# FFT mixing and squared-ReLU FFN on one core: a doubled filter block, swapped weights from DRAM, a longer lag of the inverse units and later loads

## The chip, the cores and the metric

The kernel runs on one core of one Trainium2 chip. The metric is the device time of one execution in microseconds (us). Shown in tables are the median of several runs and, apart from it, one profiled execution with its trace.

## The reference

The input x holds 8 batches of 3008 tokens with 256 channels. Each batch goes through a global filter: a real FFT along the tokens, a product with a complex filter of 1505 frequencies, and the inverse FFT. Its result is the input of an FFN with a hidden width of 2048:

```python
X = np.fft.rfft(x, axis=1)
Y = X * (filt_r + 1j * filt_i)[None, :, :]
y = np.fft.irfft(Y, n=x.shape[1], axis=1)
h = np.maximum(y.reshape(B * S, D) @ w_in, 0.0)
out = (h * h) @ w_out
```

## The kernel before

**The FFT as matrix products.** 3008 is 64 x 47. The forward transform takes two stages: `unit_a` (over 47, line 297) and `unit_b` (over 64, line 359). `unit_b` also multiplies by the filter on VectorE (line 378): the products of one psum tile with the real and the imaginary filter go side by side into `prod`. Real and imaginary parts stand in the two halves of the partitions. The inverse takes two stages more: `unit_p` (weights sSP, lines 411 and following) and `unit_y` (line 439). Between the stages of a batch the data are turned through DRAM: u is written to dU and read back as ut, ze is written to dZ and read back as zt (`write_u`, `read_u`, `read_z`).

**The FFN.** Tokens go in 47 groups of 512. A group has 8 steps. In step s, `ffn_g1` computes two of 16 hidden tiles, ScalarE takes the ReLU out of PSUM, and VectorE squares. The second product of a group runs in the 8 steps after, for the first and last group by `ffn_g2`, for all others by a seven-product scheme (`sums` on VectorE, `products` on TensorE).

**Order.** The order of the program is written by hand, and each engine works its queue in this order. TensorE, VectorE and ScalarE have one queue each. SP (SyncE) issues writes and reads of dU and dZ and the stores; POOL (GpSimd) issues the loads of x, filter and weights, and in later batches the additions prod<-prod (line 385).

**Batch 0, the prologue.** It is not interleaved with the FFN. Its first stage is done straight from wide tiles of x (`chunk_a0`), and the turn of u is done on TensorE (`turn_u`) with half of the evictions on VectorE. Twelve `unit_b` give twelve products. Every third of them (p % 3 == 0) reads the psum tile directly; the others read `ub`, a copy in f16 made by ScalarE (line 376). The products of batch 0 aren't added by POOL. Instead `unit_p0` (line 389) multiplies both halves of a product, with sSP and with `sSPx`, which is sSP with its two partition halves swapped; `sSPx` is made by four copies on VectorE (lines 699 and 700). There are six `unit_p0`, of two products each; number k-1 stands behind the `unit_b` of step k.

**The filter tile sF.** It is loaded in three blocks of columns: (0,6), (6,12) and (12,24). Partitions 0 to 63 come from DRAM, 64 to 127 hold a second copy: the real part as it is, the imaginary part with its sign turned (`turn_f`, line 241). The copy of the real part is made by VectorE for the first block (line 240) and by a transfer from SBUF to SBUF on SP for the other two (line 235).

**Later loads.** After w_in's first half, POOL issues three of the eight x loads of batch 1. `load_rest` (line 274) then makes POOL wait by copying one element of the first zt tile into `tiny`; behind this gate stand w_in's second half, five x loads and both halves of w_out. `fill` issues matmuls on zeros ahead of the first `unit_y`.

**The plan.** `fft_plan` (line 622) gives each unit of batches 1 to 7 a place in the FFN steps, in half steps. For batch 1 the numbers are steps counted from 0: `unit_a` from 1, `read_u` at 11, `unit_b` from 15 to 29, `unit_p` 4.5 later, `read_z` at 34, and `unit_y` 0 to 3 fixed at 38 to 39.5. Group 5, which begins at step 40, is the first that needs a token of batch 1. Units of batch 2 begin with `unit_b` at 47.5.

Of the kernel before, what the change touches and what calls it, by code (L numbers as in the profile page):

```python
# [102 lines left out]
def kernel(  # L103
# [73 lines left out]
    def load_x(b, k):  # L177

        c, i = divmod(k, 2)
        if i == 0:  # L180
            x16s[(b, c)] = p_x16.tile([96, 8, D], F16, tag="x16", name=f"x16_{b}_{c}")
        t = x16s[(b, c)][:, 4 * i:4 * i + 4, :]
        m = slice(8 * c + 4 * i, 8 * c + 4 * i + 4)
        if b + 1 < B:
            v = xrows[b * S:b * S + 96 * NM, :].rearrange("(p m) d -> p m d", m=NM)
            nc.gpsimd.dma_start(out=t, in_=v[:, m, :])
        else:
            v = xrows[b * S:b * S + S, :].rearrange("(p m) d -> p m d", m=NM)
            nc.gpsimd.dma_start(out=t[0:80], in_=v[0:80, m, :])
            nc.gpsimd.dma_start(out=t[80:94], in_=v[80:94, m, :])  # L190
# [34 lines left out]
    def load_f(c0, c1):  # L225

        for im, filt in enumerate((filt_r, filt_i)):
            v = filt[0:1504, :].rearrange("(j c) d -> j c d", c=47)
            a = max(c0, 1)
            nc.gpsimd.dma_start(out=sF[0:32, im, c0:c1, :], in_=v[:, c0:c1, :])  # L230
            nc.gpsimd.dma_start(out=sF[32:64, im, a:c1, :], in_=v[:, 47 - a:47 - c1:-1, :])
            if c0 == 0:
                nc.gpsimd.dma_start(out=sF[32:33, im, 0, :], in_=filt[1504:1505, :])
        if c0:
            nc.sync.dma_start(out=sF[64:128, 0, c0:c1, :], in_=sF[0:64, 0, c0:c1, :])

    def turn_f(c0, c1):

        if c0 == 0:
            nc.vector.tensor_copy(out=sF[64:128, 0, c0:c1, :], in_=sF[0:64, 0, c0:c1, :])  # L240
        nc.vector.tensor_scalar_mul(out=sF[64:128, 1, c0:c1, :], in0=sF[0:64, 1, c0:c1, :],
                                    scalar1=-1.0)

    def load_const(t, d, k):
        c = slice(12 * k, 12 * k + 12)
        nc.gpsimd.dma_start(out=t[:, c, :], in_=d.ap().rearrange("p (a b) -> p a b", b=128)[:, c, :])

    def load_win(i):
        c = slice(1024 * i, 1024 * i + 1024)
        for k in range(2):  # L250
            nc.gpsimd.dma_start(out=sWin[:, k, c], in_=moe_w_in[128 * k:128 * k + 128, c])
# [4 lines left out]
                            in_=moe_w_out.rearrange("(jt r) c -> r jt c", r=128)[:, c, :])  # L256

    FC = ((0, 6), (6, 12), (12, 24))
    for k, i in ((0, 0), (1, 0), (0, 1), (1, 1), (2, 0), (2, 1)):
        load_wide(k, i)  # L260
    nc.sync.dma_start(out=sC1, in_=dC0.ap()[:, 704:896])
    load_const(sSB, dSB, 0)
    load_f(*FC[0])
    load_const(sSP, dSP, 0)
    load_f(*FC[1])
    load_const(sSB, dSB, 1)
    load_f(*FC[2])
    load_const(sSP, dSP, 1)
    load_win(0)
    for k in range(3):  # L270
        load_x(1, k)
    sSPx = [p_u.tile([128, 12, 128], F16, tag="u", name=f"sSPx_{k}") for k in range(2)]

    def load_rest():

        tiny = const.tile([1, 1], F16, name="tiny")
        nc.gpsimd.tensor_copy(out=tiny, in_=ztiles[0][0:1, 0, 0:1])
        load_win(1)
        for k in range(3, 8):
            load_x(1, k)  # L280
        for k in range(2):
            load_wout(k)

    def fill(n):

# [73 lines left out]
    def unit_b(b, p):  # L359
        if b == 0 and p % 4 > 1:  # L360
            ps = psO(f"psB_{b}_{p}").rearrange("p a d -> p (a d)")
        else:
            ps = psF(f"psB_{b}_{p}")
        for i in range(2):
            nc.tensor.matmul(ps[:, i * D:(i + 1) * D], sSB[:, 2 * p + i, :],  # L365
                             uts[b][:, 2 * p + i, :], start=True, stop=True)
        if b == 0:
            if p == 0:
                prods["ring"] = p_y.tile([128, 5, 2, 2, D], F16, tag="yt", name="prods_0")
            prod = prods["ring"][:, p % 5]  # L370
        else:
            prod = p_prod.tile([128, 2, 2, D], F16, tag="prod", name=f"prod_{b}_{p}")
        pv = ps.rearrange("p (a d) -> p a d", d=D)
        if b == 0 and p % 3:
            ub = p_prod.tile([128, 2, D], F16, tag="prod", name=f"ub_{p}")
            nc.scalar.copy(out=ub, in_=pv)
            pv = ub
        nc.vector.tensor_mul(  # L378
            out=prod,
            in0=pv.unsqueeze(1).to_broadcast([128, 2, 2, D]),  # L380
            in1=sF[:, :, 2 * p:2 * p + 2, :])
        prods[(b, p)] = prod
        if b > 0:
            for i in range(2):
                nc.gpsimd.dma_start(out=prod[64 * i:64 * i + 64, 0],  # L385
                                    in_=prod[64 - 64 * i:128 - 64 * i, 1],
                                    accum_op=mybir.AluOpType.add)
# [234 lines left out]
    def fft_plan():  # L622

        fixed, units, moves = [], [], []
        for b in range(1, B):
            f = (b * S // TG) * SLOTS - (48 if b > 1 else 40)
            d = 0
            if b == 1:
                for n in range(4, 16):
                    fixed.append(((n if n < 8 else n + 2 if n < 12 else 2 * n - 7) + n % 2 / 2,  # L630
                                  unit_y, 0, n))
                moves.append((7.5, read_z, 0, 3))
                for a in range(16):
                    fixed.append(((1 if a < 6 else 2) + a / 2, unit_a, b, a))
                moves.append((11, read_u, b))
                d = 7
            else:
                for a in range(16):
                    if a % 2 == 0 and b > 2:
                        moves.append((f + ((-57 + 2.3 * a) if b == 3 else (-66 + 2.75 * a)),  # L640
                                      load_x, b, a // 2))
                    units.append((f + (-16 + a, -46 + 2.1 * a, -56 + 2.75 * a)[min(b, 4) - 2],
                                  unit_a, b, a))
                moves.append((f + (4 if b == 2 else -6.5), read_u, b))
            for p in range(12):
                r = 15 + 14 * p / 11 if b == 1 else 7.5 + 26.5 * p / 11 if b == 2 else -2 + 36 * p / 11
                units.append((f + r, unit_b, b, p))
                if b == 1 and 2 <= p < 10:
                    moves.append((f + r, load_x, 2, p - 2))
                units.append((f + r + (4.5 if b == 1 else 7 - 2.5 * p / 11), unit_p, b, p))  # L650
            for c in range(4):
                moves.append((f + (40 + d / 7, 43, 48, 54)[c] - d, read_z, b, c))
            for n in range(16):
                (fixed if n < 4 else units).append((f + YN[n] - d, unit_y, b, n))
        work, used, done = {}, set(), {}
        for r, *u in fixed:
            h = int(2 * r)
            used.add(h)
            work.setdefault(h, []).append(u)
        rank = (unit_b, unit_p, unit_y, unit_a)  # L660
        for r, *u in sorted(units, key=lambda u: (rank.index(u[1]), u[0])):
            after = done.get((u[0], u[1]), -1)
            h = min((h for h in range(max(int(2 * r) - 3, after + 1), int(2 * r) + 12)
                     if h not in used),
                    key=lambda h: (sum(h + i in used for i in (-2, -1, 1, 2)) > 2) * 2
                    + abs(h - int(2 * r)))
            used.add(h)
            done[(u[0], u[1])] = h
            work.setdefault(h, []).append(u)
        for r, *u in moves:  # L670
            work.setdefault(int(2 * r), []).append(u)
        return work
# [12 lines left out]
    turn_u(0, nc.scalar, nc.vector)  # L685
    turn_u(1, nc.scalar, nc.scalar)
    turn_u(2, nc.scalar, nc.vector)
    for k in range(7):
        if k < 6:
            for p in (2 * k, 2 * k + 1):  # L690
                for c in FC:
                    if c[0] == 2 * p:
                        turn_f(*c)
                unit_b(0, p)
        if 0 < k < 4:
            turn_u(k + 2, nc.scalar, nc.vector)
        if k in (0, 3):
            c = slice(4 * k, 4 * k + 12)
            nc.vector.tensor_copy(out=sSPx[k // 3][0:64], in_=sSP[64:128, c, :])
            nc.vector.tensor_copy(out=sSPx[k // 3][64:128], in_=sSP[0:64, c, :])  # L700
        if k > 0:
            unit_p0(k - 1)
    read_z(0, 0)
    read_z(0, 1)
    load_rest()
    fill(24)
    for n in range(4):
        unit_y(0, n)
    prologue[0] = False
# [53 lines left out]
```

## Time and profile before

| | |
|---|---|
| median of 3 runs | 770.87 us (770.27 to 771.49) |
| profiled execution, its span | 770.5 us |
| mean granted TensorE clock | 0.991 |
| first matmul of the FFN (psH) | 50.30 us |
| step 12 of the FFN | 74.69 us |

The profile gives, for each engine, its busy time and share of the span. PE is TensorE's matmuls, PEld its weight loads, DVE is VectorE, ACT ScalarE, POOL GpSimd, and SPq SyncE's queue. L378 is line 378 of the kernel. In the chain of work that ended last, each row is a start, a length and what the time went to, followed back from the last instruction; "DMA sF<-sF" is the time in which a transfer into sF from sF was waited for. A row of waits says who waited for what: the sum in us, how often, and the longest. A row of the timeline has start, length, engine, line, operation, and in brackets the idle time before it and what ended it. A row of windows has the stretch and its length, then busy time and number of instructions of PE, PEld, DVE, ACT and POOL, the granted clock, the DMA share and GB/s.

### The profile page before, as it was taken

The numbers are of one execution on the slowest core, as the hardware profiler recorded it, in microseconds if no ns is written. First come the engines' busy times: TensorE is split into PE (matmuls) and PEld (weight loads), VectorE is DVE, ScalarE is ACT, GpSimd is POOL, SyncE is SP. The second block draws the span as 40 slices with busy tenths as digits, with TensorE's granted clock in tenths as the row PEclk, the third lists the DMA queues.
The fourth block names the chain that finished last, engine by engine and source line by source line (L and its number), as shares of the span: only waits on it lengthen the run. The fifth ranks groups of instructions, "written<-read, shape, count | busy, mean of one in ns | idle before, by whom it ended". The sixth has DMA issues, their size and how long they took to land.

```text
span 770.5 us, 19433 instructions
## 1 busy us (share of the span) xinstructions
PE 743.0 (96%) x8150; PEld 545.0 (71%) x8150; DVE 639.0 (83%) x711; ACT 569.8 (74%) x839; POOL 190.9 (25%) x267
## 2 busy tenths in 40 slices
PE   6687999999999999999999999999999999999997
PEld 4444666777777777877778777787777777777776
DVE  4736897899879898898988889798989989888783
ACT  3456778787887877788877887878876777777773
POOL 6220571043303232223212323143311222000000
PEclk9799999999999999999999999999999999999999
DMA  8979698566676457754576465765447334321011
GB/s 167 219 168 178 154 177 218 185 135 138 126 199 146 101 115 152 214 129 86 132 189 160 101 128 110 202 142 119 100 105 210 90 76 97 97 72 54 29 56 56
DMA packets 106591, 102.69 MB, mean 133 GB/s; under 512 B 9880, under 2 KB 94424, under 8 KB 105608
## 3 DMA queue, kind: packets, MB, share of 16 engines
q1 hardware_dynamic: 80760, 72.49, 31.5%
q0 software_dynamic: 25600, 28.79, 25.8%
q8 instruction: 64, 1.05, 0.6%
q14 instruction: 23, 0.19, 0.1%
q10 hardware_dynamic: 144, 0.18, 0.1%
HBM read 57.77 MB, written 48.23 MB: 138 GB/s over the span
## 4 chain that ended last, share of the span: by engine, by line
PE 80%; DVE 9%; DMA 8%; issue 2%; POOL 1%; ACT 0%; SPq 0%; DVEq 0%; ACTq 0%; POOLq 0%
PE psH L483 36%; PE psX L596 19%; PE psY L596 14%; DVE prod L378 3%; DVE h L494 2%; PE psY L453 2%; PE psA L304 2%; DMA sWout<-in_moe_w_out_dram 2%; PE psB L365 2%; PE psP L417 2%; PE psO L503 2%; DMA sSB<-cSB 1%; DMA sF<-sF 1%; DMA zt<-dZ 1%; DMA sF<-in_filt_r_dram 1%
## 5 line engine op out<-in xcount | busy, mean ns | idle before, releaser
L487 ACT ACTIVATE h<-psH 128x1024 f16<-128x1024 f32 x376 | 385.1, 1024 | 154.2 <-PE psH L483 151.8
L483 PE MATMUL psH<-yt,sWin 128*128 128x512 f16 (+7 forms) x1728 | 386.9, 351 | 0.4 <-ACT yt L460 0.3
L494 DVE TENSOR_TENSOR h<-h 128x2048 f16<-128x2048 f16 (+1 forms) x192 | 229.8, 1197 | 41.2 <-ACT h L487 40.9
L385 POOL DMA_DIRECT2D prod<-prod x168 | 139.7, 977 | 428.1 <-DVE prod L378 383.8
L483 PEld LDWEIGHTS <-sWin 128*128 128x128 f16 x1728 | 152.1, 98 | 99.8 <-issue 4.4
L596 PEld LDWEIGHTS <-sum 128*128 128x128 f16 x2880 | 177.5, 98 | 19.8
L596 PEld LDWEIGHTS <-h 128*128 128x128 f16 x2160 | 133.7, 98 | 21.3
L378 DVE TENSOR_TENSOR prod<-psB,sF 128x1024 f16<-128x1024 f32 x84 | 102.3, 1219 | 16.9 <-PE psB L365 16.8
L596 PE MATMUL psX<-sT,sum 128*128 128x128 f16 x1440 | 102.4, 219 | 0.0
L596 PE MATMUL psY<-sT,sum 128*128 128x128 f16 x720 | 69.6, 219 | 0.0
L308 ACT CAST u<-psA 96x512 f16<-96x512 f32 x96 | 55.7, 580 | 2.5 <-PE psA L304 2.1
L572 DVE TENSOR_TENSOR sum<-sum,h 128x2048 f16<-128x2048 f16 x45 | 55.0, 1222 | 1.0
L462 DVE CAST yt<-psY 128x376 f16<-128x376 f32 x62 | 33.8, 544 | 26.2 <-PE psY L453 26.2
L596 PE MATMUL psY<-sWout,h 128*128 128x128 f16 x720 | 54.9, 219 | 0.0
L596 PE MATMUL psX<-sT,h 128*128 128x128 f16 x720 | 54.9, 219 | 0.0
L575 DVE TENSOR_TENSOR sum<-h 128x2048 f16<-128x2048 f16 x45 | 54.8, 1217 | 0.0
L596 PE MATMUL psY<-sWout,sum 128*128 128x128 f16 x720 | 54.7, 219 | 0.0
L578 DVE TENSOR_TENSOR sum<-h,sum 128x2048 f16<-128x2048 f16 x45 | 54.7, 1216 | 0.0
L569 DVE TENSOR_TENSOR sum<-h 128x2048 f16<-128x2048 f16 x45 | 54.7, 1216 | 0.0
L419 ACT CAST ze<-psP 128x512 f16<-128x512 f32 x84 | 48.9, 584 | 0.2 <-PE psP L417 0.2
L453 PEld LDWEIGHTS <-zt 112*128 112x128 f16 x512 | 33.5, 97 | 21.8 <-issue 7.6
L596 PE MATMUL psX<-sWout,h 128*128 128x128 f16 x720 | 47.5, 219 | 0.0
(73 smaller groups left out, 595.2 us busy)
## 6 DMA issues: line engine op xcount, KB each, us to landing
zt<-dZ SPq DMA_DIRECT2D x64, 192.0 KB
dU<-u SPq DMA_DIRECT2D x28, 384.0 KB
prod<-prod POOLq DMA_DIRECT2D x168, 64.0 KB, 2.8
dZ<-ze SPq DMA_DIRECT2D x28, 384.0 KB
x<-in_x_dram POOLq DMA_DIRECT2D x48, 192.0 KB, 5.1
ut<-dU SPq DMA_DIRECT2D x7, 1024.0 KB
out_dram<-top SPq DMA_DIRECT2D x31, 128.0 KB
out_dram<-bot SPq DMA_DIRECT2D x31, 128.0 KB
```

The lines of the kernel that those rows point to most:

```text
L308: nc.scalar.copy(out=o, in_=pv)
L378: nc.vector.tensor_mul(out=prod, in0=pv.unsqueeze(1).to_broadcast([128, 2, 2, D]), in1=sF[:, :, 2 * p:2 * p + 2, :])
L385: nc.gpsimd.dma_start(out=prod[64 * i:64 * i + 64, 0], in_=prod[64 - 64 * i:128 - 64 * i, 1], accum_op=mybir.AluOpType.add)
L453: nc.tensor.matmul(ps[:, 94 * jj:94 * jj + 94], zt[:, 4 * (g % 2) + jj, dt * 128:(dt + 1) * 128], sSY, start=True, stop=True)
L483: nc.tensor.matmul(ps[:, i, o:o + n], sWin[:, dt, jt * 128:(jt + 1) * 128], yts[b][:, dt, r:r + n], start=(dt == 0), stop=(dt == 1))
L487: nc.scalar.activation(out=h2[:, 2 * s:2 * s + 2, :], in_=ps, func=AF.Relu)
L494: nc.vector.tensor_mul(out=v, in0=v, in1=v)
L569: nc.vector.tensor_add(out=t, in0=a21, in1=a22)
L572: nc.vector.tensor_sub(out=t, in0=f[5], in1=a11)
L575: nc.vector.tensor_sub(out=t, in0=a11, in1=a21)
L578: nc.vector.tensor_sub(out=t, in0=a12, in1=f[6])
L596: nc.tensor.matmul(o[:, t, :], f[p][:, q, 128 * t:128 * t + 128], sg["w"][p][:, q, :], start=(m == 0 and p in (1, 2)), stop=(q == 7), skip ...
```

## The change

- Filter block (6,12): the real part is doubled by VectorE in `turn_f`, and SP's transfer is left for block (12,24) only.
- `sSPx` is loaded from DRAM, by two loads of 64 partitions for each half, issued by POOL just behind the half of sSP. sSP's first half moves behind filter block (6,12). VectorE's four copies go.
- In batch 0 only every sixth product reads PSUM directly (p % 6), so products 3 and 9 go through `ub`.
- `unit_p0(k - 2)` in place of `unit_p0(k - 1)`, between the two `unit_b` of a step; the loop has 8 steps.
- The three early x loads of batch 1 go. POOL has two gates: the first waits for the last part of ze (column 21 of 24) and lets w_in's second half go; the second waits for the first zt tile as before, and lets four x loads, w_out, and four x loads more go. `fill(22)` in place of `fill(24)`.
- Batch 1: `unit_a` two steps later (3 + a/2, and 4 + a/2 from a = 8), `read_u` at 12.5, `unit_b` from 16.5 to 30, `unit_p` 4 behind it, the first `read_z` at 34.5. Batch 2: `read_u` 1.5 later, `unit_b` from 49, with the end where it was.

```diff
-        if c0:
+        if c0 > 6:
             nc.sync.dma_start(out=sF[64:128, 0, c0:c1, :], in_=sF[0:64, 0, c0:c1, :])
     def turn_f(c0, c1):
-        if c0 == 0:
+        if c0 < 12:
             nc.vector.tensor_copy(out=sF[64:128, 0, c0:c1, :], in_=sF[0:64, 0, c0:c1, :])
...
+    sSPx = [p_u.tile([128, 12, 128], F16, tag="u", name=f"sSPx_{k}") for k in range(2)]
+    def load_sp(k):
+        load_const(sSP, dSP, k)
+        v = dSP.ap().rearrange("p (a b) -> p a b", b=128)[:, 12 * k:12 * k + 12, :]
+        for i in (0, 64):
+            nc.gpsimd.dma_start(out=sSPx[k][i:i + 64], in_=v[64 - i:128 - i])
...
     load_f(*FC[0])
-    load_const(sSP, dSP, 0)
     load_f(*FC[1])
+    load_sp(0)
     load_const(sSB, dSB, 1)
     load_f(*FC[2])
-    load_const(sSP, dSP, 1)
+    load_sp(1)
     load_win(0)
-    for k in range(3):
-        load_x(1, k)
...
-    def load_rest():
-        tiny = const.tile([1, 1], F16, name="tiny")
-        nc.gpsimd.tensor_copy(out=tiny, in_=ztiles[0][0:1, 0, 0:1])
-        load_win(1)
-        for k in range(3, 8):
+    tiny = const.tile([1, 2], F16, name="tiny")
+    def load_rest(k):
+        if k == 0:
+            nc.gpsimd.tensor_copy(out=tiny[:, 0:1], in_=zes[0][0:1, NC - 3, 0:1])
+            load_win(1)
+            return
+        nc.gpsimd.tensor_copy(out=tiny[:, 1:2], in_=ztiles[0][0:1, 0, 0:1])
+        for k in range(4):
             load_x(1, k)
         for k in range(2):
             load_wout(k)
+        for k in range(4, 8):
+            load_x(1, k)
...
-        if b == 0 and p % 3:
+        if b == 0 and p % 6:
             ub = p_prod.tile([128, 2, D], F16, tag="prod", name=f"ub_{p}")
...
-                    fixed.append(((1 if a < 6 else 2) + a / 2, unit_a, b, a))
-                moves.append((11, read_u, b))
+                    fixed.append(((3 if a < 8 else 4) + a / 2, unit_a, b, a))
+                moves.append((12.5, read_u, b))
...
-                moves.append((f + (4 if b == 2 else -6.5), read_u, b))
+                moves.append((f + (5.5 if b == 2 else -6.5), read_u, b))
...
-                r = 15 + 14 * p / 11 if b == 1 else 7.5 + 26.5 * p / 11 if b == 2 else -2 + 36 * p / 11
+                r = 16.5 + 13.5 * p / 11 if b == 1 else 9 + 25 * p / 11 if b == 2 else -2 + 36 * p / 11
...
-                units.append((f + r + (4.5 if b == 1 else 7 - 2.5 * p / 11), unit_p, b, p))
+                units.append((f + r + (4 if b == 1 else 7 - 2.5 * p / 11), unit_p, b, p))
...
-                moves.append((f + (40 + d / 7, 43, 48, 54)[c] - d, read_z, b, c))
+                moves.append((f + (40 + d / 14 * 3, 43, 48, 54)[c] - d, read_z, b, c))
...
-    for k in range(7):
+    for k in range(8):
         if k < 6:
             for p in (2 * k, 2 * k + 1):
                 for c in FC:
                     if c[0] == 2 * p:
                         turn_f(*c)
+                if k > 1 and p % 2:
+                    unit_p0(k - 2)
                 unit_b(0, p)
         if 0 < k < 4:
             turn_u(k + 2, nc.scalar, nc.vector)
-        if k in (0, 3):
-            c = slice(4 * k, 4 * k + 12)
-            nc.vector.tensor_copy(out=sSPx[k // 3][0:64], in_=sSP[64:128, c, :])
-            nc.vector.tensor_copy(out=sSPx[k // 3][64:128], in_=sSP[0:64, c, :])
-        if k > 0:
-            unit_p0(k - 1)
+        if k > 5:
+            unit_p0(k - 2)
     read_z(0, 0)
     read_z(0, 1)
-    load_rest()
-    fill(24)
+    load_rest(0)
+    load_rest(1)
+    fill(22)
```

More of the change, by code (lines that the diff above doesn't have):

```diff
@@ L263 @@
     load_f(*FC[0])
-    load_const(sSP, dSP, 0)
     load_f(*FC[1])
+    load_sp(0)
     load_const(sSB, dSB, 1)
     load_f(*FC[2])
-    load_const(sSP, dSP, 1)
+    load_sp(1)
     load_win(0)
-    for k in range(3):
-        load_x(1, k)
-    sSPx = [p_u.tile([128, 12, 128], F16, tag="u", name=f"sSPx_{k}") for k in range(2)]
-    def load_rest():
-        tiny = const.tile([1, 1], F16, name="tiny")
-        nc.gpsimd.tensor_copy(out=tiny, in_=ztiles[0][0:1, 0, 0:1])
-        load_win(1)
-        for k in range(3, 8):
+    tiny = const.tile([1, 2], F16, name="tiny")
[6 more added lines that the diff above has]
+        for k in range(4):
             load_x(1, k)
```

## The prediction

> **What bounds the kernel now.** I read the busy table first, then the chain of work that ended last over the first 140 us, then the waits and the timeline of the places it names, then windows for the clock. TensorE is busy for nearly all of the span, so what can be won lies where it stands still:
>
> ```profile
> PE 743.0 (96%) x8150; PEld 545.0 (71%) x8150; DVE 639.0 (83%) x711; ACT 569.8 (74%) x839; POOL 190.9 (25%) x267
> ```
>
> The chain says where: transfers, VectorE and ScalarE carry most of it until 69.63, with TensorE only from 35.89 to 41.75; from 69.63 to 81 it is matmuls alone. Its columns are start, length, what.
>
> ```profile
> 18.30 6.51 DMA sF<-in_filt_r_dram
> 24.88 7.27 DMA sF<-sF
> ...
> 32.27 1.82 DVE prods L378 x2
> 34.10 0.60 DVE ut L350
> 34.71 0.55 DVE sSPx L699
> 35.28 0.57 DVE sSPx L700
> ...
> 41.75 0.60 ACT ze L404
> 42.37 0.70 DVE ze L405
> ...
> 43.62 3.07 DMA zt<-dZ
> ...
> 46.75 0.18 POOL tiny L277
> ...
> 46.98 5.93 DMA sWin<-in_moe_w_in_dram
> ...
> 53.20 16.39 DMA sWout<-in_moe_w_out_dram
> 69.63 1.03 PE psO L503 x8
> ```
>
> Three things stand in it: the duplicate of the last filter block (lands at 32.2), the products and inverse units after it (ze complete at 43.06), and the load of w_out. The waits of TensorE up to 140 us name the same, and a fourth, batch 1's first output unit:
>
> ```profile
> PE psP L399 <- DVE prods L378: 2.3, 2, 1.8
> PE psP L399 <- DVE sSPx L700: 2.2, 2, 2.0
> PE psO L503 <- DMA sWout<-in_moe_w_out_dram: 1.7, 1, 1.7
> ```
> ```profile
> 131.15 0.33 PE L453 MATMUL psY<-sC,zt 112*128 112x94 f16 x4 [0.85 <-DMA zt<-dZ]
> ```
>
> **What the skill says.** "TensorE: Matmul & The Clock Gate", Part 1: the clock is either full or half, judged in windows of about 3.4 us. The trace agrees; the windows below (share of PE, then clock) show 1.49 of 3.41 busy followed by half clock, 2.15 of 3.41 at half clock not yet releasing it, 3.04 of 3.40 releasing it. "VectorE: DVE Perf Modes", Mode 1x: PSUM operands run at the baseline rate; the product from psB takes 1224 ns, from the f16 copy ub 684. "DMA: Bandwidth & Descriptors", Latency and other measured facts: first byte about 0.6 us by the hardware queue, and memory latency that grows under load. Here it grows more: 7.27 us for the loaded 384 KB duplicate, 3.07 for the quiet zt read.
>
> ```profile
> 17.57:20.98 3.41, 1.49 (x17) 1.08 (x15) 3.12 (x5) 2.66 (x6) 3.30 (x6) 1.00 1.02 175
> 24.40:27.80 3.40, 3.04 (x19) 2.21 (x17) 1.17 (x2) 2.48 (x4) 0.51 (x1) 0.50 1.16 280
> 34.63:38.04 3.41, 2.15 (x11) 1.54 (x12) 3.00 (x5) 0.44 (x1) 0.00 (x0) 0.50 0.59 172
> 44.87:48.28 3.41, 2.13 (x12) 0.90 (x10) 0.00 (x0) 0.00 (x0) 1.48 (x4) 1.00 0.74 194
> ```
>
> **Part 1: up to the duplicate.** Doubling block (6,12) on VectorE costs one copy of 0.55 (as L240) and drops a 192 KB SyncE transfer, for which product 3 stood from 24.45 to 26.68. That is no gain by itself: everything until product 6 waits for the duplicate of (12,24) at 32.2 anyway, where VectorE idled 0.99 already. So these edits count only through when that lands (D). Its source is queued on POOL behind two more 192 KB loads (swapped weights) than before; a 384 KB sSP load landed 0.8 behind its predecessor, so I charge 0.8 to 1.1. Against it: filter block 1 is issued 0.5 to 0.9 earlier, ahead of sSP instead of behind it, and the 192 KB duplicate no longer shares the engines. Net +0.3: issue 25.2, and with the same 7.3 under load D = 32.5 (31.8 if the engines are lighter, 33.5 if nothing compensates). The four added issues take POOL 0.57 each, beside other loads. Batch 1's first three x loads leave this stretch; they landed 10.5 us after issue at 33 to 36, on no chain, so that is nothing here and a cost in part 3.
>
> **Part 2: D to the first output unit.** VectorE after D, before: 32.27 to 40.43, 8.16, with two sSPx copies (1.11), product 9 from PSUM, and 1.45 idle for ub. After: product 6 takes 1.15 net of overlap, five from ub 0.6 each, one ut copy 0.65: 4.8. ScalarE gains ub 3 and ub 9 (0.59 each) in idle time (it idled 4.68 before 37.60). The inverse units lag one step more, so TensorE no longer stops for a product just made: unit 3 can start at D+1.8 = 34.3; at half clock a unit lasts 1.7, so unit 3 to 35.9, its 1.0 eviction, ub 11 to 37.45, product 11 at 38.1, unit 5 from 38.2. TensorE is busy nearly all of 34.63 to 38.04, so I take full clock from there: unit 5 ends 39.1, the two ze halves take 0.05+0.60+0.04+0.69, ze complete at 40.5 instead of 43.06: **-2.5** (39.9 to 42.5 from D and the clock).
>
> The first gate now lets w_in's second half start when ScalarE's half of that ze is written, 0.7 before ze is complete. Behind it on POOL stand only the later gate and loads. Its packets come 2 us after issue (46.98 to 49), 512 KB at roughly 3 us, thus beside the zt reads, whose second half is the one the output unit waits for (48.81, 5.75 after ze complete). Quiet they land in 3 us, the reads of 50.09 under load in about 6. I charge **+0.7** (0 to 2). First output matmul at 47.0. Two fills fewer (0.43 us) are off the path, since TensorE waits 1.8 for zt there.
>
> **Part 3: group 0 of the FFN.** Before, step 0 starts at 50.30, step 8 at 64.46, step 10 at 70.72, step 12 at 74.69: 24.4 in all. w_out's second half landed at 69.6 because five x loads and w_in were ahead of it. Now the later gate goes at 45.3 and four x loads are ahead: w_in is nearly done. Before, 2496 KB (w_in 512, x 960, w_out 1024) took 46.98 to 69.58, 110 KB per us. At this pace x 0 to 3 and w_out (1792 KB) are there at 61.6, needed from step 8 on at 62: the wait at 67.7 to 69.6 (**-1.9**) goes. The price: x 4 comes after w_out, at 63.3, and unit_a 8 sits in TensorE's order in step 8 at 62.7: +0.6. unit_a is moved two steps on: steps 0 to 7 hold eight units instead of twelve, two ScalarE casts fewer of 0.58 on the engine that sets these steps (-1.15); steps 10 and 11 get four units more of 0.22 (+0.9). Sum -1.9+0.6-1.15+0.9 = **-1.6** (0 to -3). read_u one and a half steps later: u complete about 72, ut read from 76, wanted at 80; the stores that it passes on SyncE have three buffers and are waited for by nobody near.
>
> **Part 4: batch 1 and 2 later.** From unit_b 0 to 11 VectorE is busy without a gap (81.36 to 113.64): 12 products of 1.22, squares, sums. The same work now begins 1.5 steps later, in 13.5 steps instead of 14, with one free step lost but less stolen before: **+0.3** (0 to 1). The last unit_p moves half a step (33.5 to 34), read_z 34 to 34.5, the output unit stays at 38. Its ze was ready at 121.8 but its write was issued at 123.51, behind SyncE's stores, so of the 1.08 of half a step I charge **+0.5** (0 to 1.5) on top of the 0.85 wait. The x loads of batch 2 keep their places relative to unit_b: nothing, POOL runs at 25%. Batch 2's moves fall where TensorE has no wait: 0 (-0.3 to +0.3).
>
> Sum: -2.5 +0.7 -1.6 +0.3 +0.5 = -2.6. The profiled span is 770.5 against 770.87 in the median run, so 768.3.
>
> **Rivals.**
> - *More than forecast, about 765.6*: no contention for zt (0 instead of +0.7), D at 31.8 (-0.7), no added wait for x 4 (-0.6) nor at 131 (-0.5): -5.2 with half of the rest. For it: DMA is 0.2 to 0.44 busy at 36 to 44. Against: all at once. 0.13.
> - *Hidden anyway, about 770.4*: the gain before 47 is lost. Fill ends near 44.2 and the first output matmul comes at 47 or later, so the window 44.87 to 48.28 may hold about 1.2 busy instead of 2.13, under the 1.49 that was followed by half clock; steps 0 to 2 then run at 1.7 instead of 1.02, +1.4, together with D at 33.3 (+0.8): -0.4. 0.19.
> - *Slower, about 772.7: the second half of batch 1's x.* TensorE runs in order, so unit_a 8 holds back everything at step 8. The pace of 110 KB per us comes from a stretch with two 384 KB writes of u beside it, and a w_out half took 14.8 and 16.4 us to land. If x 4 lands after 67.0, its wait is over 4.3, and the kernel is over 1.5 slower; that is a pace of 91 KB per us. At 69 it gives +1.8. For it: DMA share is above 1.2 at 58 to 66. Against: two u writes start later than before. 0.18.
> - *The change doesn't do what it says*: the copies, loads and placements are all written out by hand and each engine keeps its order, so I give this none; what may fail to come is the full clock at 38, and that is in the range.
>
> **How the numbers follow.** Forecast 0.50 at 768.3 (its own range 766.6 to 769.8), the rivals 0.13, 0.19 and 0.18. What a measurement here can tell from no change is 0.2%, 1.5 us. Faster: 0.48 of the forecast, 0.13, and 0.04 of the hidden case, 0.65. Slower: 0.17 of the third rival and 0.01 of the hidden one, 0.18. Same 0.17. The range 765.5 to 771.9 leaves out some 0.05 below and most of the slower case above.
>
> **What would show it.** In the changed profile: no sSPx copies; product 6 starting at 32 to 33.5; ze complete near 40.5; first psY at about 47; no wait for sWout in step 9; at most a short wait for x in step 8; step 12 near 70.9 instead of 74.7; the zt wait at step 38 a little above 0.85. Wrong if the duplicate lands after 34, if psY starts after 48.8, or if TensorE waits for x over 4 us.

## The result and the profile after

The changed kernel takes 777.56 us in the median of four runs (776.29 to 779.60), against 770.96 for the kernel before beside it: a ratio of 1.0089 (95% interval 1.0065 to 1.0112). The forecast was 768.3 us, with a range of 765.5 to 771.9. It is slower, not faster, and lies above the range.

The profiled execution is the slowest of the four (span 777.8 us at a mean clock of 0.986; the other three had spans of 774.5 to 775.9 at 0.989). It is some 2 us longer than they are, so one of its stretches at half clock may be missing in the others; which one isn't known, since only this execution has a trace.

First the busy line of the changed kernel's page: TensorE is busy some 2 us longer than before, at the same share of the span. So the loss isn't to be read here.

```profile
PE 744.9 (96%) x8148; PEld 546.5 (70%) x8148; DVE 636.7 (82%) x708; ACT 570.8 (73%) x841; POOL 192.8 (25%) x272
```

Next the chain of work that ended last in the changed kernel, from the third filter block to the first output matmul (start, length, what; here and in the chains below pieces under 0.2 us are left out):

```profile
19.15 8.72 DMA sF<-in_filt_r_dram
27.95 8.19 DMA sF<-sF
36.27 1.24 DVE prods L389
37.64 1.86 PE psP L410 x8
39.50 0.43 PE psB L376 x2
39.93 3.43 PE psP L410 x16
43.38 0.59 ACT ze L415
44.00 0.70 DVE ze L416
44.72 5.34 DMA dZ<-ze
50.07 3.08 DMA zt<-dZ
53.29 0.33 PE psY L464 x4
```

The duplicate lands at 36.2, not at 32.2. The work behind it has become shorter as meant. Then a row stands in the chain that had not been there: 5.34 us of writing ze to DRAM. Before, that write took about 2.5: SyncE's queue issued it at 43.08, and the read that waits for it at 45.58.

```profile
43.08 0.36 SPq L406 DMA_DIRECT2D dZ<-ze  x1
...
45.58 1.25 SPq L435 DMA_DIRECT2D zt<-dZ  x3
```

The waits of TensorE up to 145 us in the changed kernel say the same from its side; no row for sWout is left among them. Columns: the sum in us, how often, the longest.

```profile
PE psY L464 <- DMA zt<-dZ: 7.1, 2, 5.0
PE psP L410 <- DVE prods L389: 5.8, 1, 5.8
...
PE psP L410 <- DMA sSPx<-cSP: 1.6, 1, 1.6
```

The second of the two waits of psY is the one of batch 1 at step 38, 2.02 us where it was 0.85. The timeline of the changed kernel has it in brackets:

```profile
137.67 0.33 PE L464 MATMUL psY<-sC,zt 112*128 112x94 f16 x4 [2.02 <-DMA zt<-dZ]
```

Windows of the changed kernel show what both waits of psY cost beyond themselves (stretch, length, busy time of PE, PEld, DVE, ACT, POOL, granted clock, DMA share, GB/s):

```profile
50.14:53.55 3.41, 0.26 (x6) 0.29 (x7) 0.00 (x0) 0.00 (x0) 1.53 (x4) 1.00 0.89 220
53.55:56.96 3.41, 3.35 (x24) 1.97 (x22) 1.10 (x2) 0.94 (x2) 3.41 (x6) 0.50 1.04 162
...
135.50:138.90 3.40, 1.38 (x23) 1.14 (x23) 1.78 (x4) 1.50 (x2) 0.00 (x0) 1.00 1.06 318
138.90:142.30 3.40, 3.40 (x25) 2.51 (x24) 0.57 (x2) 1.66 (x3) 0.00 (x0) 0.50 0.25 73
```

A window with little TensorE work is followed by one at half clock, at the start of the FFN and again behind batch 1's output unit. The kernel before had neither.

The profiled spans differ by 7.3 us (770.5 and 777.8). By stage, from the marks of both traces (rounded; "h of step 0" is ScalarE's ReLU of that step, taken at its end):

| stage | before | after | difference | forecast |
|---|---|---|---|---|
| start to product 6 | 32.27 | 36.27 | +4.0 | +0.3 |
| product 6 to ze complete | 10.79 | 8.42 | -2.4 | -2.8 |
| ze complete to first psY | 5.8 | 8.6 | +2.8 | +0.7 |
| first psY to the end of h of step 0 | 3.68 | 4.93 | +1.2 | 0 |
| h of step 0 to h of step 12 | 24.09 | 23.65 | -0.45 | -1.6 |
| h of step 12 to h of step 36 | 50.35 | 50.44 | +0.1 | +0.3 |
| h of step 36 to h of step 40 | 9.55 | 12.30 | +2.75 | +0.5 |
| rest | | | -0.8 | 0 |

### The profile page after: what moved, and what is told of

It is laid out like the page before. It is cut to its first block, busy times and chain, and to the rows that moved or that the text cites. A ratio compares the mean times of both kernels' runs of the same rounds, so it can differ in the third digit from the quotient of the medians.

```text
span 777.8 us, 19439 instructions
## 1 busy us (share of the span) xinstructions
PE 744.9 (96%) x8148; PEld 546.5 (70%) x8148; DVE 636.7 (82%) x708; ACT 570.8 (73%) x841; POOL 192.8 (25%) x272
## 4 chain that ended last, share of the span: by engine, by line
PE 81%; DVE 8%; DMA 7%; ACT 1%; POOL 1%; issue 1%; SPq 0%; DVEq 0%; ACTq 0%; POOLq 0%
PE psH L494 37%; PE psX L607 19%; PE psY L607 14%; PE psY L464 3%; PE psA L315 2%; DVE prod L389 2%; DVE h L505 2%; PE psB L376 2%; PE psP L428 2%; PE psO L514 1%; DMA sSB<-cSB 1%; DMA dZ<-ze 1%; DMA sF<-in_filt_r_dram 1%; ACT h L498 1%; DMA sF<-sF 1%
## 5 line engine op out<-in xcount | busy, mean ns | idle before, releaser
L464 PE MATMUL psY<-sC,zt 112*128 112x94 f16 x512 | 43.4, 208 | 8.4 <-DMA zt<-dZ 7.1
```

Of the source, the lines that this page charges most:

```text
L464: nc.tensor.matmul(ps[:, 94 * jj:94 * jj + 94], zt[:, 4 * (g % 2) + jj, dt * 128:(dt + 1) * 128], sSY, start=True, stop=True)
```

## Experiments

The theory after the result had three costs: the early half of w_in shares the DMA engines with the write of ze and starves the output unit (W); the loads of the swapped weights delay the filter block (S); the later plan of batch 1 lengthens the wait at step 38 (P). The rival: one of these carries all, or it is something else, the missing early x loads above all. Times are medians; a ratio is to the kernel before on the same chip, with its 95% interval; it isn't the quotient of the two medians. The kernel before took 771.6 to 772.1 there.

### Parts taken out of the changed kernel

**e1_sspx_dve**: the changed kernel, with the swapped weights copied by VectorE again.

```diff
-            nc.gpsimd.dma_start(out=sSPx[k][i:i + 64], in_=v[64 - i:128 - i])
...
+        if k in (0, 3):
+            c = slice(4 * k, 4 * k + 12)
+            nc.vector.tensor_copy(out=sSPx[k // 3][0:64], in_=sSP[64:128, c, :])
+            nc.vector.tensor_copy(out=sSPx[k // 3][64:128], in_=sSP[0:64, c, :])
```

> The changed kernel with the swapped weights made by VectorE's four copies again and their four loads taken out of POOL's queue; all else as changed. Theory 1 (the four 64-partition loads delay the last filter block): the block's real half lands about 3 us earlier (near 25 instead of 27.9), its duplicate lands at 32.3 to 33.3 instead of 36.2, first psY near 50.5 instead of 53.3, and the kernel gains 2 to 3 us on the changed one (near 775). Rival (the delay comes from the moved order or from DMA load in general): duplicate still after 35, gain under 1 us.

Measured: 777.02 us, 1.0064 (1.0042 to 1.0085). Product 6 starts at 33.13 instead of 36.27, so S is real in its place. With the copies back on VectorE ze is complete 1.9 us earlier (42.81 and 44.69). But psY still comes at 53.15 (53.29 in the changed kernel): the write of ze then takes longer still, 7.1 us, and eats all of it. In this trace an earlier ze gains nothing behind W; in time the interval of e1 overlaps that of the changed kernel (1.0065 to 1.0112).

**e2_win_zt**: the changed kernel, with w_in's second half behind the gate on zt and two x loads.

```diff
-            nc.gpsimd.tensor_copy(out=tiny[:, 0:1], in_=zes[0][0:1, NC - 3, 0:1])
-            load_win(1)
...
-        for k in range(4):
+        for k in range(2):
+            load_x(1, k)
+        load_win(1)
+        for k in range(2, 4):
```

> The changed kernel with w_in's second half behind the gate on zt instead of the gate on ze (order: x 0, x 1, w_in, x 2, x 3, w_out, x 4 to 7). Theory 2 (w_in's load slows the last write of ze and the zt reads): the last write takes about 2.5 us instead of 5.3, first psY comes 5.7 to 6 us after ze is complete instead of 8.6, so near 50.5, the clock stays full at the start of the FFN, and the kernel gains 2 to 4 us (near 774.5). Rival (the write is slow whatever POOL loads, since the same queue holds earlier writes): psY still 8 us after ze, gain under 1 us.

Measured: 777.32 us, 1.0070 (1.0052 to 1.0089). The write of ze is back at 2.35 us and psY comes at 48.26, 5 us earlier than in the changed kernel; but TensorE then stands 1.6 us for w_in and step 12 ends at 78.65, only 3.2 us earlier. In the profiled run (774.08) this is a gain, in the median of 16 runs it is none. The edit moved w_in behind two x loads too, so this run doesn't isolate W.

**e3_both**: e1 and e2 together.

```diff
-            nc.gpsimd.dma_start(out=sSPx[k][i:i + 64], in_=v[64 - i:128 - i])
-            nc.gpsimd.tensor_copy(out=tiny[:, 0:1], in_=zes[0][0:1, NC - 3, 0:1])
...
```

> Both of the two edits above at once. If the two delays are separate and add up: duplicate near 33, first psY near 47.5 to 48, kernel near 771.5 to 772.5, that is 5 to 6 us under the changed one. Rival (they hide one another): no better than the better of the two alone by 1 us.

Measured: 780.09 us, 1.0100 (1.0056 to 1.0144), a miss: no repair, rather worse. Its wait at step 38 was 2.91 us, the longest of all kernels, and steps 36 to 40 took 13.3 us. It sent me to single parts added to the kernel before.

### Parts put alone into the kernel before

**e4_compute**: block (6,12) doubled by VectorE, p % 6, the longer lag.

```diff
-        if c0:
+        if c0 > 6:
...
-        if b == 0 and p % 3:
+        if b == 0 and p % 6:
...
+                if k > 1 and p % 2:
+                    unit_p0(k - 2)
```

> The kernel before with only the compute edits: block (6,12) doubled by VectorE, products 3 and 9 through ub, inverse units two steps behind. Loads, gates, fills and plan as before. Theory: from the landing of the last duplicate (still 32 to 32.5) to ze complete 9 to 9.6 us instead of 10.8, so ze near 41.6, first psY 47.3, and the kernel is 1 to 1.8 us faster than before (769.2 to 770). Rival (the tail is hidden behind something else, the clock or the ze writes): within 0.5 us of before.

Measured: 770.86 us, 0.9989 (0.9971 to 1.0007). psY comes at 47.55, 1.3 earlier than before: a gain of the right kind, about half the size, and less at the end of the kernel than a measurement can tell. Its trace has half clock at the start of the FFN, which that of the kernel before has not, and h of step 0 ends only 0.8 earlier.

**e5_plan**: the later plan of batch 1.

```diff
-                r = 15 + 14 * p / 11 if b == 1 else
+                r = 16.5 + 13.5 * p / 11 if b == 1 else
...
-                units.append((f + r + (4.5 if b == 1
+                units.append((f + r + (4 if b == 1
...
-                moves.append((f + (40 + d / 7, 43, 48, 54)[c] - d, read_z, b, c))
+                moves.append((f + (40 + d / 14 * 3, 43, 48, 54)[c] - d, read_z, b, c))
```

> The kernel before with only the later plan of batch 1: unit_b from 16.5, unit_p 4 behind, first read_z at 34.5 (and read_u of batch 2 at 5.5, which the shifted order needs). unit_a, loads and prologue as before. Theory 3 (the half step that read_z loses is paid at the first output unit of batch 1, more when the standstill lets the clock fall): steps 12 to 36 take the same 50.4 us, the wait for zt there grows from 0.85 to 1.5 to 2.9 us, the kernel is 0.7 to 2.5 us slower than before. Rival (the wait is set by SyncE's queue, not by the plan): wait below 1.5, within 0.5 us of before.

Measured: 776.31 us, 1.0056 (1.0035 to 1.0078). It can't be read as P: read_u of batch 2 had moved too, without its unit_b, and TensorE waited 2.3 us for the transfer ut<-dU of batch 2. **f1_plan_clean** repeats it with batch 2's unit_b moved as in the change.

```diff
 # on top of e5
...
-                                     7.5 + 26.5 * p / 11 if b == 2
+                                     9 + 25 * p / 11 if b == 2
...
```

> The kernel before with only the later plan of batches 1 and 2 as the change has it: unit_b of batch 1 from 16.5 and of batch 2 from 49, unit_p 4 behind, first read_z at 34.5, read_u of batch 2 at 5.5; unit_a, loads and prologue as before. Unlike e5_plan, batch 2's unit_b doesn't stand ahead of its ut. Theory 3 (the half step that read_z loses is paid at batch 1's first output unit): wait for zt there 1.5 to 2.9 us instead of 0.24 to 1.53 with the plan of before, kernel 0.7 to 2.5 us slower than before. Rival (e5_plan's loss was batch 2's ut alone): within 0.5 us of before.

Measured: 772.71 us, 1.0007 (0.9994 to 1.0020). The later plan alone costs nothing that can be told from zero. Its wait at step 38 is 1.72 us.

**e6_win_early**: w_in's second half behind a gate on ze, nothing else.

```diff
...
+        nc.gpsimd.tensor_copy(out=tiny[:, 0:1], in_=zes[0][0:1, NC - 3, 0:1])
+        load_win(1)
         nc.gpsimd.tensor_copy(out=tiny[:, 1:2], in_=ztiles[0][0:1, 0, 0:1])
-        load_win(1)
```

> The kernel before with only w_in's second half let go by the ze gate instead of the zt gate; all else as before. Theory 2: the last ze write takes 5 to 7 us instead of 2.5, first psY comes 8.5 to 10.5 us after ze is complete instead of 5.75, that is at 51.5 to 53.5, and the kernel is 2.5 to 4.5 us slower than before (the wait for w_out gives back up to 1.9 of it). Rival (only together with the changed queue of loads): psY within 1 us of 48.8.

Measured: 774.84 us, 1.0037 (1.0026 to 1.0048). This is W by itself, some 2.9 us. Its chain has the long write again, ahead of the reads of zt:

```profile
41.04 0.70 DVE ze L406
41.76 5.25 DMA dZ<-ze
47.08 3.14 DMA zt<-dZ
50.35 0.33 PE psY L454 x4
```

**e7_sspx_load**: only the loads of the swapped weights.

```diff
...
-    load_const(sSP, dSP, 0)
+    load_sp(0)
...
-    load_const(sSP, dSP, 1)
+    load_sp(1)
...
-            nc.vector.tensor_copy(out=sSPx[k // 3][0:64], in_=sSP[64:128, c, :])
-            nc.vector.tensor_copy(out=sSPx[k // 3][64:128], in_=sSP[0:64, c, :])
```

> The kernel before with only the swapped weights loaded by POOL (two loads of 64 partitions behind each half of sSP) in place of VectorE's four copies. Theory 1: the last filter block's real half lands 2.5 to 3.5 us later than 24.82, product 6 starts at 35 to 36 instead of 32.27, VectorE saves 1.1 behind it, first psY 1.5 to 2.5 us later, kernel 1 to 2.5 us slower than before. Rival (the loads take what batch 1's early x loads took, nothing lands later that matters): within 0.5 us of before or faster.

Measured: 771.63 us, 1.0000 (0.9982 to 1.0017). S alone is a draw, and its chain shows the two sides of it:

```profile
19.77 6.66 DMA sF<-in_filt_r_dram
26.49 7.89 DMA sF<-sF
34.50 1.24 DVE prods L386
```

Product 6 starts 2.2 us later than before, and without the copies the rest takes 5.9 us to product 11 instead of 8.2. What the loads delay, VectorE saves behind.

**f3_load_order**: x 3, w_out, x 4 to 7, with the later unit_a and read_u.

```diff
-        for k in range(3, 8):
-            load_x(1, k)
+        load_x(1, 3)
         for k in range(2):
             load_wout(k)
+        for k in range(4, 8):
+            load_x(1, k)
...
-                    fixed.append(((1 if a < 6 else 2) + a / 2, unit_a, b, a))
-                moves.append((11, read_u, b))
+                    fixed.append(((3 if a < 8 else 4) + a / 2, unit_a, b, a))
+                moves.append((12.5, read_u, b))
```

> The kernel before with only the later x loads and unit_a: x 3, then w_out, then x 4 to 7 behind the one gate; unit_a two steps later as the change has it, read_u at 12.5. Theory 4 (w_out's early landing takes the wait of 1.7 us away, but steps 10 and 11 with three extra units each cost it back): w_out lands before 64, steps 0 to 12 take 22.5 to 24 us against 24.1, kernel within 1 us of before on either side. Rival as I predicted (1.6 us gained): 769 to 770.5 with before at 772.

Measured: 773.21 us, 1.0011 (0.9999 to 1.0024). w_out lands at 58.1 and 61.0 and is waited for by nobody; yet nothing is won. Part of it is lost to a wait of 2.0 us for ut, since unit_b still began at step 15; the changed kernel doesn't have this wait, so f3 is no clean measure of the order alone.

### In the changed kernel again, one repair after the other

**g1_x_early** gives the early x loads 0 to 2 back. **g2_x_early_win_zt** also takes the gate on ze away. **g3_x_win_spx** also copies the swapped weights on VectorE.

```diff
 # g1
+    for k in range(3):
+        load_x(1, k)
-        for k in range(4):
-            load_x(1, k)
+        load_x(1, 3)
 # g2, on top of g1
-            nc.gpsimd.tensor_copy(out=tiny[:, 0:1], in_=zes[0][0:1, NC - 3, 0:1])
-            load_win(1)
...
+        load_win(1)
         load_x(1, 3)
 # g3, on top of g2: the edit of e1
...
```

> The changed kernel with batch 1's x 0 to 2 loaded in the prologue behind w_in's first half, as before; behind the zt gate x 3, w_out, x 4 to 7. w_in's second half still goes at the ze gate. Theory 5 (part of the loss is x 0 to 3 landing only at 56 to 59, which together with the stands of the output unit starts the FFN at half clock): step 0 to 12 takes 22.5 to 23.5 us, 0.5 to 2 us faster than the changed kernel (775.5 to 777). Rival (x was early enough, step 3 needs it at 60): no difference.

> The same with w_in's second half behind the zt gate: early w_in undone without late x. Theories 2 and 5 together: first psY near 50 (product 6 still late because of the weight loads), no half clock at the FFN's start, 3 to 5 us faster than the changed kernel (772.5 to 774.5). Rival (the changed kernel's rest is slow by itself, as e2 and e3 with late x suggest): 776 or more.

> The same, and the swapped weights by VectorE's copies: all that is left of the change is the compute edits, block 1 ahead of sSP, the order x 3, w_out, x 4 to 7, unit_a two steps later and the later plan of batch 1 and 2. If the parts add up (compute -0.75, load order +0.8, plan +0.5, each measured alone): within 1 us of before. Rival (these parts cost more together than alone): 1.5 us or more above before.

Measured: 779.63 us, 1.0096 (1.0068 to 1.0123); 774.91 us, 1.0029 (1.0014 to 1.0045); 773.80 us, 1.0028 (1.0015 to 1.0041). Giving the early x loads back doesn't help as long as the gate on ze stands. With the gate away it may: g2 and g3 are clear of e2 and e3, but those two also have w_in behind two x loads, so this isn't shown. Taking the gate away is worth 4.7 us in one step, and the intervals of g1 and g2 don't overlap. The chains of g1 and then of g2 around the write:

```profile
44.92 0.70 DVE ze L417
45.64 5.39 DMA dZ<-ze
51.05 3.24 DMA zt<-dZ
54.43 0.47 PE psY L465 x4
```
```profile
43.75 0.70 DVE ze L416
44.47 2.40 DMA dZ<-ze
46.89 3.12 DMA zt<-dZ
50.14 0.33 PE psY L464 x4
```

The swapped weights on VectorE (g3) bring no more than the interval holds, as e7 said. But g3 is still 2.2 us slower than the kernel before, where the sum of the parts left in it would have put it within 1 us: its rival, that they cost more together than alone, fits better.

**h1_z_back** puts unit_p and read_z of batch 1 back to their earlier places behind the later unit_b, to see whether the half step of read_z makes the wait at step 38.

```diff
-                units.append((f + r + (4 if b == 1
+                units.append((f + r + (3.5 if b == 1
...
-                moves.append((f + (40 + d / 14 * 3, 43, 48, 54)[c] - d, read_z, b, c))
+                moves.append((f + (40 + d / 7, 43, 48, 54)[c] - d, read_z, b, c))
```

> g3 (the change without early w_in, late x and the weight loads) with batch 1's unit_p 3.5 behind unit_b and its first read_z back at 34; unit_b stays at 16.5 to 30. If the rest of the loss is paid at batch 1's first output unit: wait for zt there 0.3 to 1.5 us instead of 2.3, no half clock behind it, steps 36 to 40 in 9 to 10.2 us instead of 12.7, kernel 1.5 to 2.5 us faster than g3 and within 0.8 us of before. Rival (unit_a and the load order are the rest): no gain on g3.

Measured: 775.89 us, 1.0053 (1.0037 to 1.0068), a miss. The wait stays:

```profile
133.79 0.42 PE L461 MATMUL psY<-sC,zt 112*128 112x94 f16 x4 [2.35 <-DMA zt<-dZ]
```

The last write of ze is now issued 8.3 us before TensorE is due to read it (6.3 in g3), but from that write to the first psY it takes 10.6 us instead of 8.6. The time won in the plan is lost in the transfers. SyncE's queue shows one difference: in h1 a write dU<-u of 384 KB is issued 0.5 us ahead of that write of ze (122.68 and 123.16), in g3 3.9 us ahead (120.29 and 124.21). No run moves it, so this isn't shown to be the cause.

### Away from the transfer

What stands in the chain of the prologue before and after is the duplicate sF<-sF, 7.3 and 8.2 us for 384 KB. **e8_all_dve** is e4 with the third block doubled by VectorE as well.

```diff
-        if c0 > 6:
-            nc.sync.dma_start(out=sF[64:128, 0, c0:c1, :], in_=sF[0:64, 0, c0:c1, :])
-        if c0 < 12:
+        if True:
```

> The compute-only kernel (e4) with the third filter block doubled by VectorE too, so that no transfer stands between the filter's landing and product 6. If the duplicate is what holds the prologue: copy of about 1.05 and sign turn of 0.95 follow the landing of the block's last part at 27.4, product 6 starts at 28.5 to 29.5 instead of 32.5, ze complete near 38 to 39, first psY near 44, kernel 3 to 4.5 us faster than before (766.5 to 768.5). Rival (the time returns in the load of w_out and w_in, which starts from the same place but shares the engines with nothing less): psY early but the FFN's step 12 gains under 1.5 us.

Measured: 767.46 us, 0.9944 (0.9922 to 0.9965), faster than both kernels. In the timeline of its VectorE one copy of 0.95 us (L238) stands in place of the transfer; the sign turn (L239) was there before. Product 6 starts at 29.55:

```profile
27.62 0.95 DVE L238 COPY sF<-sF 64x3072 f16<-64x3072 f16 x1
28.50 0.95 DVE L239 TENSOR_SCALAR sF<-sF 64x3072 f16<-64x3072 f16 x1
29.55 1.22 DVE L376 TENSOR_TENSOR prods<-psB,sF 128x1024 f16<-128x1024 f32 x1
```

**f2_z_earlier** is e8 with unit_p of batch 1 a step earlier (3.5) and read_z at step 33; **f4_spx1_load** is e8 with the second half of the swapped weights loaded.

```diff
 # f2, on top of e8
-                units.append((f + r + (4.5 if b == 1
+                units.append((f + r + (3.5 if b == 1
-                moves.append((f + (40 + d / 7, 43, 48, 54)[c] - d, read_z, b, c))
+                moves.append((f + (40, 43, 48, 54)[c] - d, read_z, b, c))
 # f4, on top of e8
+        nc.gpsimd.dma_start(out=sSPx[1][i:i + 64], in_=...)
-        if k in (0, 3):
+        if k == 0:
```

> The kernel with all three filter blocks doubled by VectorE (e8) with batch 1's unit_p 3.5 steps behind unit_b and its first read_z at 33 instead of 34. If the half steps of read_z are paid for at batch 1's first output unit: no wait for zt there (under 0.3 us), 0.3 to 1.2 us faster than e8_all_dve, 5 to 6 us faster than before. Rival (moving unit_p closer to unit_b makes TensorE wait for the additions of POOL): step 12 to 36 grows over 50.7 us and nothing is gained.

> e8 with the second half of the swapped weights loaded by POOL behind sSP's second half, and VectorE's two copies after product 7 gone. No filter block stands behind these two loads. If the copies are on the path there: products end 1.1 us earlier than in e8 (36.49), first psY near 43.6, 0.5 to 1.2 us faster than e8. Rival (the loads land after 31, and unit 3 waits for them): no gain.

Measured: 767.16 us, 0.9931 (0.9918 to 0.9945), and 767.76 us, 0.9938 (0.9918 to 0.9958). In f2 the wait at step 38 is gone, in e8 it was 0.24; neither differs from e8 by more than the intervals. f4 shows the write of ze once more: ze is complete 2.3 us earlier than in e8 (36.80 and 39.08), but the write, issued while the last of the early x loads was landing (37.4), took 4.4 us, and psY comes at 44.51 (44.65 in e8).

**h2_repaired** is h1 with e8's edit, the later unit_b of batch 1 kept.

```diff
 # on top of h1
-            nc.sync.dma_start(out=sF[64:128, 0, c0:c1, :], in_=sF[0:64, 0, c0:c1, :])
-        if c0 < 12:
+        if True:
```

> h1 with the third filter block doubled by VectorE too: the change kept in its compute edits, unit_a, load order and later unit_b, and mended where the runs before found a cost. If the causes named are all: product 6 near 29.5, first psY near 45, 3.5 to 4.5 us faster than h1, so 767 to 768.5 with before at 771.8, level with e8_all_dve. Rival (late unit_a and the load order cost something that only shows once the prologue is short): 769.5 or more.

Measured: 769.90 us, 0.9983 (0.9967 to 0.9998): the change with its repairs is a little faster than the kernel before, and slower than e8, whose plan is the old one. It is a miss against its expectation and lies where its rival put it. What it has besides e8's edits (later unit_a, the load order, later unit_b, filter block 1 ahead of sSP) costs the rest; the runs don't divide it. Its wait at step 38 is 2.42 us.

## Why the prediction was wrong

Two terms of the sum were sized wrong and carry the larger part of the miss: the early half of w_in, put at +0.7, and the issue of the duplicate, put at +0.3. Both of the prediction's signs of being wrong in the prologue came: the duplicate landed after 34 (36.2), and psY started after 48.8 (53.3). In total time only the first of the two is shown to cost.

**Part 1, "Net +0.3": it failed, by 3.7 us.** The step was the issue of the duplicate at 25.2; it was issued at 27.95. The chains give the parts of it: POOL issues the last load of the filter's real part at 19.15 instead of 18.30, and this load takes 8.72 instead of 6.51. The two extra loads ahead of it landed 1.0 and 0.8 us behind their predecessors, 1.8 together, where I charged 0.8 to 1.1. Against that I had set 0.5 to 0.9 for the earlier issue of filter block 1. That block did land 0.9 earlier (20.5, before 21.4), but sSP's first half, moved behind it, took the next 1.7 and still stood ahead of the last block. The Trainium skill, "DMA: Bandwidth & Descriptors", Rules for kernel authors, says that two transfers to disjoint halves of the partitions serialize, and the landings here agree: 1.8 us for the 384 KB in two, 1.7 for the 384 KB of sSP in one just ahead of them. And the duplicate took 8.2 instead of 7.3. In total time the loads cost less than in their place: e7 shows a draw, since the copies saved behind pay for them.

**Part 2, D to ze, "-2.5": its mechanism held, but for the clock.** From product 6 to ze the changed kernel takes 8.42 us where 8.0 was forecast (10.79 before). Full clock, which the sum took from 38.04 on, 5.5 us after the duplicate's landing D, didn't come in time, so nothing of this gain is the clock's: behind the wait for product 6 TensorE ran at half clock from 36.5 to 43.3, through all of the last inverse units (16 matmuls in 3.43 us), as it had before.

```profile
36.50:39.90 3.40, 2.26 (x11) 1.65 (x12) 3.40 (x6) 0.36 (x1) 0.00 (x0) 0.50 0.29 85
39.90:43.30 3.40, 3.40 (x18) 2.35 (x16) 1.28 (x2) 2.15 (x3) 0.00 (x0) 0.50 0.24 77
```

**Part 2, early w_in, "+0.7 (0 to 2)": the mis-sized term that costs most.** I priced contention for the reads of zt, and took 40.5 plus 5.75 as given otherwise. Contended was the write of ze ahead of them. Over the 19 traces it took 2.3 to 2.5 us in the 14 in which no load of POOL was in flight, 4.4 in f4, and 5.3 to 7.1 in the four with the early half of w_in (the changed kernel, e1, e6, g1). The reads kept their 3.1. The 7.27 and 3.07 us that the prediction sets side by side are two transfers of different size and path (384 KB within SBUF, 192 KB from DRAM), so they don't give the price of load either. The skill, same page, section Queues, rings and completion order, says that each DMA engine goes round between the queues that have work for it, packet by packet. If the two shared evenly, a write of 256 KB from SP beside 512 KB from POOL would take about twice as long as alone, an estimate from that page: 5.3 for 2.4 agrees, 7.1 in e1 is more. From ze to psY it makes 8.6 us instead of 5.8. Then, as the rival "hidden anyway" had it, half clock at the start of the FFN (+1.2). That isn't the early load's alone: all four traces with it have half clock there, but so have six of the other 15, f1 among them, whose prologue is that of the kernel before. e6 gives +2.9 for the early load alone, g1 and g2 4.7 inside the changed kernel. It doesn't decide the sign by itself: g2, without it, is still slower than the kernel before (1.0029).

**Part 3, "-1.6": half right.** The wait for w_out is gone, and to step 10 the FFN gains 2.2 us (18.1 from the h of step 0, 20.3 before). Then the moved unit_a cost more than the +0.9: in the timeline of the changed kernel's ScalarE, h of steps 10, 11 and 12 are 2.7 and 2.8 us apart, 1.9 before.

```profile
75.31 1.02 ACT L498 ACTIVATE h<-psH 128x1024 f16<-128x1024 f32 x1 [0.68 <-PE psH L494]
...
78.03 1.02 ACT L498 ACTIVATE h<-psH 128x1024 f16<-128x1024 f32 x1 [0.85 <-PE psH L494]
...
80.85 1.02 ACT L498 ACTIVATE h<-psH 128x1024 f16<-128x1024 f32 x1 [0.84 <-PE psH L494]
```

That is +1.7, so -0.45 is left. It comes with the moved unit_a: h of step 10 to h of step 12 takes 5.54 us in all ten kernels that have it, f3 among them, and 3.81 in all nine that don't. These ten have the changed order of loads too, but in the chain of the changed kernel no load is waited for in these steps. The wait for x 4 that the slower rival feared didn't come.

**Part 4: "+0.3" was too much, "+0.5" right in size and wrong in what follows.** The stretch of VectorE cost nothing. The last write of ze of batch 1 was issued 6.6 us before its reader was due in the mean of the nine kernels with the whole later plan, and 7.2 in the seven with the old one: 0.6 later, as charged. With the transfers a little longer too (8.6 and 8.4 from write to psY), the wait became 1.55 to 2.91 us instead of 0.24 to 1.53. In three of the nine traces half clock followed (the changed kernel, e3, g3), and steps 36 to 40 took 2.75 to 3.7 us more than before; in the other six they took 0.7 to 1.3 more. The prediction had put no term for the clock there.

**What stays open.** The parts alone come to -0.8 (e4), +2.9 (e6), 0 (e7), +0.5 (f1) and +0.8 (f3), +3.4 in all, all but e6 within their intervals of zero; the whole is +6.6. The runs show 1.9 of the rest: W costs 4.7 in the changed kernel and 2.9 alone. What then remains is 1.3, or some 2 us more, since f3's part holds a wait for ut that the changed kernel hasn't. Taken from the other side: with early w_in, late x and the weight loads out (g3), 2.2 us of loss are left, the sum of the compute edits, filter block 1 ahead of sSP, unit_a, the load order and the later plan; the runs don't divide it. Half clock after the wait at step 38 fits, but no run takes it away alone. Why transfers around step 36 stretch when read_z moves forward in h1 and h2 was not settled either.

## What to carry to other kernels

Before letting a load go earlier, ask which small transfer on the critical path will run beside it, writes ahead of reads included. Here that one paid, and the trace in which it ran alone didn't show the price. Time won ahead of an output unit counts only if the transfer into that unit ends earlier too: in e1 ze was complete 1.9 us earlier than in the changed kernel, and psY came at the same time. Where a transfer within SBUF stands in the chain for 7 us, see whether an engine that stands idle there can copy it: here 0.95 us of VectorE brought the clearest gain in the study (e8 against e4, h2 against h1).

## What the hardware showed that I had not expected

- TensorE fell to half clock after standing 2.02 us (1.38 us of 3.40 busy in the window). The skill, "TensorE: Matmul & The Clock Gate", Why this matters for your kernels, warns of gaps of over about 3 us. Waits of 2.02, 2.33, 2.35, 2.42 and 2.91 us at step 38 were followed by half clock here (the changed kernel, g3, h1, h2, e3), those of up to 1.92 were not, and one of 2.15 (g2) wasn't either.
- The duplicate of 384 KB within SBUF took 7.3 us before and 8.2 after, beside POOL's loads (6.9 to 8.9 in the chains of the other runs), VectorE's copy of the same block 0.95.
- The last write of ze of batch 0, 256 KB from SP, took 2.3 to 2.5 us while POOL had no load in flight, and 5.3 to 7.1 beside a load of 512 KB.
